# Convolution work kept out of the step that ends a run of the second matmul and the step behind it

## The chip, the cores and the metric

The kernel runs on one core of one Trainium2 chip. The metric is the device time of one execution in microseconds (us). Five engines work beside each other and meet through semaphores: TensorE (PE in the profile; PEld is its weight load), VectorE (DVE), ScalarE (ACT), GpSimd (POOL) and SyncE (SP, which issues the DMAs).

## What is computed

Two layers, each a gated long convolution (H3) and a squared-ReLU MLP, both behind a layernorm, on 2048 tokens of 1024 features, with 3584 hidden features, in float32:

```python
# x: [1, 2048, 1024]; layernorm over the features, no scale
def A(q, k, v, shift_k, ssm_k, ssm_D):
    kv = short_causal_conv(k, shift_k) * v          # 4 taps
    y = irfft(rfft(pad(kv)) * rfft(pad(ssm_k)))     # causal conv along the 2048 tokens, per feature
    return q * (y + kv * ssm_D)
def B(x, w1, b1, w2, b2):
    h = relu(x @ w1 + b1) ** 2
    return h @ w2 + b2
for _ in range(2):
    x = x + A(layernorm(x), k, v, shift_k, ssm_k, ssm_D)
    x = x + B(layernorm(x), w1, b1, w2, b2)
```

The convolution's result before the gate depends on k, v and the filter alone. It is the same for both layers, so it is computed once.

## The kernel before

**Matmuls.** The tokens are four blocks of 512. `ORDER` lists seven units of (layer, block): (0,0), (1,0), (0,1), (0,2), (1,1), (0,3), (1,2), the last of which takes blocks 2 and 3 of layer 1 together. A float32 product is three matmuls with a high and a low half of each operand (`mm3`, L355 to L358). The high half of a weight tile is a cast on ACT (L1112), the low half a subtraction on DVE or POOL (L1120), made some three steps ahead of its use; a hidden tile is treated the same way (L1599, L1602, L1604 on ACT, the low half at L1607 on DVE).

**Steps.** A unit is a list of steps. A step uses one weight tile: "m1" (first matmul) or "m2" (second). It has 12 matmuls of 512 columns, or of 256 columns where only half of the block's tokens are ready: the half steps at the turn from unit 0 to unit 1 are the last m2 steps of unit 0, from step 106, and the first m1 steps of unit 1, steps 134 to 157. Seven m2 steps make a run that sums in four PSUM banks. The last step of a run (`end`) is followed, one step later, by the eviction `evict` (L1727): four DVE additions into the sums in SBUF. At the turn, `add_b2` adds the second bias to the sums, four instructions on POOL (L1850).

**Convolution.** It is cut into blocks of 256 tokens and computed by a transform in short pieces. Its work is spread between the steps of units 0 to 4 in two ways:

- `fwd_tick` advances two generators. `fwd_x` makes one feature group's transform of the input: three shifted multiply-adds on DVE (L386), the product with v (L388), transposes on PE (L441) a fixed number of ticks later, then further matmuls and DVE combinations (L402, L423, L424, L428). `fwd_g` does the like for the filter (L485, L486, L489, L490, L504, L505).
- `prod_stream` (`pds`) makes the products of the transforms: a multiply on POOL (L546, by 3 to 8 blocks wide), a sum over it on DVE (L550), and for each group a fold (L696) and a butterfly (L700, L701) on POOL, then the inverse matmuls (L616) and a copy on ACT. Each call of `next(pds)` yields the work just issued in a unit of its own (0.384 for a product of 3 blocks, 0.512 for one of 4), or None where it waits for a forward transform or a buffer.

**Pacing.** In each step, `rate` is the work that should be issued (from `pace`), a tenth of it in half steps; `owed` sums it up. Products are issued until `todo`, at most 1.06 times the rate (`BURST`), is used up; one that is begun counts in full, so any `todo` above nothing issues one product. A None issues a forward tick instead. Beside that, `fowed` grows by `FWD_RATE` in each full step (1.4 in unit 0), and each whole one is a forward tick. No rule looks at whether a step ends a run. Every engine takes its instructions in the order in which the loop issues them.

Of the kernel before, what the change touches and what calls it, by code (L numbers as in the profile page):

```python
# [22 lines left out]
NT = T // P  # L23
# [24 lines left out]
W_AFTER = 4  # L48
AHEAD_0 = 4
BURST = 1.06  # L50
FIN = "GGG"
PACE_SLACK = {1: 74, 3: 10}
PACE_TO = {1: 2}
# [198 lines left out]
def tile_h3_mlp(ctx: ExitStack, tc: tile.TileContext, q, kT, vT, shk, ssmT, ssmD, w1, b1, w2, b2,  # L252
# [280 lines left out]
    def fwd_tick():  # L533
        for g in streams:
            next(g, None)
# [4 lines left out]
    def prod_stream():  # L540
# [11 lines left out]
        def fin(st, sm, sb, g, k):  # L552
            s = sm.rearrange("p k j c -> p k (j c)")
            E = ENG[FIN[sb - 1]]
            if k == 0:
# [1593 lines left out]
    owed = town = 0.0  # L2149
    fowed = 0.0  # L2150
# [3 lines left out]
    top = 0  # L2154
    cur_u = -1
    ready = set(ALL)

    def close_conv(nb):
        while nb not in done:
            if next(pds) is None:  # L2160
                fwd_tick()

    for s, (k, u, c, a, i, tts, w) in enumerate(steps):
# [58 lines left out]
        elif k == "w2":  # L2222
# [10 lines left out]
            if i == done_at - 1:  # L2233
                end = c == len(WCH) - 1
# [8 lines left out]
        else:  # L2243
            turned = direct[u] and c == NCH - 1 and tts[0] > 0 and a == 1
            begin, end = (s in opens, s in closes) if turned else (i == 0, i == FC - 1)
# [60 lines left out]
        rate = pace.get(u, 100) * (PREP_PACE if busy else 1.0)  # L2306
        if len(tts) < NT:
            rate *= 0.1
        owed += rate
        todo = min(owed, BURST * rate)  # L2310
        while todo > 0:
            x = next(pds, 0)
            if x == 0:
                owed = todo = 0
            elif x is None:
                fwd_tick()
                todo = 0
# [1 line left out]
                todo -= x  # L2319
                owed -= x  # L2320
        fowed += FWD_RATE.get(u, 2) * (0.0 if busy or len(tts) < NT else 1.0)
        while fowed >= 1:
            fowed -= 1
            fwd_tick()
    lag.flush()


# [47 lines left out]
```

## Time and profile before

| | us |
|---|---|
| time, median of 3 runs | 2676.86 (2676.43 to 2679.94) |
| the profiled execution | 2678.26 |
| its span in the trace | 2676.5 |
| granted clock of PE, mean | 0.995 |

How to read the profile: a row of the timeline gives the start, the duration, the engine, the line of the kernel, the operation, output and inputs, and in brackets how long the engine stood idle before it and what it waited for. A row of the groups by shape gives the count, then the total busy time and the mean duration in ns, then the idle time before the instructions of the group. The list of waits gives total us, times and the longest. A row of the windows gives the stretch, its length, then the busy time of each engine with the number of instructions, the granted clock of PE, the DMA engines' share and GB/s.

### The profile page before, as it was taken

The page shows a single profiled execution, that of the slowest core. Times are in us where ns is not written, and L with a number is a line of the kernel's source. Part 1 is how long each engine was busy: PE and PEld are TensorE (multiplying, and loading weights), DVE is VectorE, ACT ScalarE, POOL GpSimd, SP SyncE. Part 2 cuts the span into 40 slices and gives each one's busy share as a digit, 9 for nine tenths or more (in the row PEclk, how much of TensorE's full clock was granted, in tenths as well). Part 3 has the DMA queues.
Part 4 walks back from the last instruction along what each step waited for, and adds up shares of the span by engine and source line. Part 5 has one row for each costly group of instructions (what it writes and reads, how often), then busy time and mean ns, then how long its engine had stood idle before and what let it go on. Part 6 is the DMA issues. An engine that isn't in the chain of part 4 may idle for free.

```text
span 2676.5 us, 36110 instructions
## 1 busy us (share of the span) xinstructions
PE 2623.3 (98%) x12388; PEld 2198.9 (82%) x12388; DVE 1980.9 (74%) x2848; ACT 1133.8 (42%) x1931; POOL 1034.8 (39%) x683
## 2 busy tenths in 40 slices
PE   8899999899999999999999999999999999999999
PEld 7888787788888888888888888888788778888887
DVE  7878888789987777779777775456778767777553
ACT  5454344444444333343333422345444585454442
POOL 2436665255542645427554175000100217536111
PEclk9999999999999999999999999999999999999999
DMA  8799898689989998788987888689889798878653
GB/s 255 250 316 310 295 302 282 234 290 369 353 296 312 317 333 298 276 299 305 339 303 253 300 295 305 207 264 315 300 295 307 264 338 254 264 252 312 231 195 121
DMA packets 380265, 763.16 MB, mean 285 GB/s; under 512 B 44064, under 2 KB 159408, under 8 KB 377008
## 3 DMA queue, kind: packets, MB, share of 16 engines
q1 hardware_dynamic: 380080, 760.85, 83.3%
q8 instruction: 98, 1.61, 0.2%
q14 instruction: 87, 0.71, 0.1%
HBM read 583.49 MB, written 177.21 MB: 284 GB/s over the span
## 4 chain that ended last, share of the span: by engine, by line
PE 80%; DMA 6%; DVE 4%; ACT 2%; issue 1%; POOL 1%; SPq 0%; DVEq 0%; POOLq 0%; ACTq 0%
PE p L356 24%; PE p L357 24%; PE p L358 24%; PE pt L358 2%; PE pt L356 2%; PE pt L357 2%; DMA whl<-wd_m 2%; DMA wr<-w 1%; DMA wd_m<-whl 1%; DVE whl L1120 1%; DMA yt<-yd 0%; PE pt L412 0%; PE pt L441 0%; DMA cx<-xd 0%; PE pt L616 0%
## 5 line engine op out<-in xcount | busy, mean ns | idle before, releaser
L546 POOL TENSOR_TENSOR cp<-cx,cg 128x384 f32<-128x384 f32 (+5 forms) x288 | 542.6, 1897 | 569.2 <-DVE sm L550 374.6
L356 PE MATMUL p<-xh,whl 128*128 128x512 f32 (+1 forms) x1504 | 577.0, 384 | 6.3 <-DMA whl<-wd_m 5.7
L358 PE MATMUL p<-xh,whl 128*128 128x512 f32 (+1 forms) x1504 | 572.9, 381 | 3.3 <-DVE whl L1120 2.8
L357 PE MATMUL p<-xl,whl 128*128 128x512 f32 (+1 forms) x1504 | 572.8, 381 | 0.4 <-DVE xl L1515 0.4
L1112 ACT CAST whl<-wr 128x512 fp32r<-128x512 f32 x546 | 332.4, 619 | 466.4 <-PE p L358 275.1
L1120 DVE TENSOR_TENSOR whl<-wr,whl 128x512 fp32r<-128x512 f32 x486 | 426.2, 888 | 131.0 <-ACT whl L1112 130.3
L356 PE MATMUL p<-whl,rh 128*128 128x512 f32 x1204 | 477.1, 396 | 4.9 <-DMA whl<-wd_m 4.3
L357 PE MATMUL p<-whl,rh 128*128 128x512 f32 x1204 | 472.1, 392 | 2.5 <-POOL whl L1120 1.4
L358 PE MATMUL p<-whl,rl 128*128 128x512 f32 x1204 | 471.5, 392 | 0.0
L356 PEld LDWEIGHTS p<-xh,whl 128*128 128x128 f32 x1504 | 283.4, 188 | 61.1 <-DMA whl<-wd_m 2.5
L358 PEld LDWEIGHTS p<-xh,whl 128*128 128x128 f32 x1504 | 283.3, 188 | 58.3 <-DVE whl L1120 3.0
L357 PEld LDWEIGHTS p<-xl,whl 128*128 128x128 f32 x1504 | 283.5, 188 | 52.7 <-DVE xl L1515 0.6
L1607 DVE TENSOR_TENSOR rl<-wr,rh 128x512 fp32r<-128x512 f32 x140 | 142.2, 1016 | 177.9 <-ACT rh L1604 177.7
L356 PEld LDWEIGHTS p<-whl,rh 128*128 128x128 f32 x1204 | 227.9, 189 | 53.4 <-DVE fg L1716 3.3
L1120 POOL TENSOR_TENSOR whl<-wr,whl 128x512 fp32r<-128x512 f32 x60 | 87.3, 1458 | 475.9 <-ACT whl L1112 447.7
L357 PEld LDWEIGHTS p<-whl,rh 128*128 128x128 f32 x1204 | 227.9, 189 | 50.2 <-DVE whl L1120 2.7
L358 PEld LDWEIGHTS p<-whl,rl 128*128 128x128 f32 x1204 | 227.6, 189 | 48.0
L550 DVE TENSOR_REDUCE sm<-cp 128x128 f32<-128x384 f32 (+5 forms) x288 | 249.4, 874 | 10.2 <-POOL cp L546 10.2
L1599 ACT ACTIVATE wr<-p,b1t 128x512 f32<-128x512 f32 x138 | 95.3, 690 | 367.2 <-PE p L358 366.2
L1727 DVE TENSOR_TENSOR acc<-p,acc 128x512 f32<-128x512 f32 x152 | 100.0, 686 | 81.0 <-PE p L358 80.9
L696 POOL TENSOR_TENSOR sm<-sm 128x512 f32<-128x512 f32 x48 | 68.7, 1431 | 134.0 <-DVE sm L550 128.5
L356 PE MATMUL p<-whl,tq 128*128 128x512 f32 x276 | 107.4, 389 | 0.0
(393 smaller groups left out, 4280.5 us busy)
## 6 DMA issues: line engine op xcount, KB each, us to landing
whl<-wd_m SPq DMA_DIRECT2D x318, 512.0 KB, 5.5
wr<-w SPq DMA_DIRECT2D x442, 256.0 KB, 5.7
wd_m<-whl SPq DMA_DIRECT2D x70, 512.0 KB, 6.0
wr<-td SPq DMA_DIRECT2D x112, 256.0 KB, 5.0
cx<-xd SPq DMA_DIRECT2D x48, 512.0 KB, 5.9
cg<-gd SPq DMA_DIRECT2D x48, 512.0 KB, 6.8
tq<-hd SPq DMA_DIRECT2D x24, 1024.0 KB, 7.3
gd<-fg SPq DMA_DIRECT2D x72, 256.0 KB, 5.9
```

The lines of the kernel that those rows point to most:

```text
L356: PE.matmul(o, lh, rh, start=start, stop=False)
L357: PE.matmul(o, lh, rl, start=False, stop=False)
L358: PE.matmul(o, ll, rh, start=False, stop=stop)
L546: G.tensor_mul(pr.rearrange("p c i -> p i c"), xt[:, 0:j + 1], gt[:, j::-1])
L550: V.tensor_reduce(sm[:, ty, jj], st["pr"], axis=AX.X, op=OP.add)
L696: E.tensor_add(s[:, 1:3], s[:, 1:3], s[:, 0:1].to_broadcast([P, 2, s.shape[2]]))
L1112: A.copy(t[:, 0], raws[n]["t"])
L1120: ENG[e[n % len(e)]].tensor_sub(t[:, 1], raws[n]["t"], t[:, 0].bitcast(F32))
L1599: A.activation(r, st["o"], AF.Relu, bias=b1t[:, st["f"]:st["f"] + 1])
L1607: V.tensor_sub(st["lo"], st["r"]["t"], st["hi"].bitcast(F32))
L1727: V.tensor_add(accs[tt][:, d], o, accs[tt][:, d])
```

## The change

A new set `rest` holds the steps that follow the end of an m2 run. In the step that ends a run, and in the step behind it, nothing is issued from `pds`, and no forward tick is made. In the other full steps the limit is 1.3 times the rate instead of 1.06 where work is owed, and at most three forward ticks are made from `fowed`. In half steps the limit stays at 1.06 times their rate.

```diff
+CATCH = 1.3
...
+    rest = set()
...
         owed += rate
-        todo = min(owed, BURST * rate)
+        still = k == "m2" and end or s in rest
+        if k == "m2" and end:
+            rest.add(s + 1)
+        todo = 0.0 if still else min(owed, (BURST if len(tts) < NT else CATCH) * rate)
         while todo > 0:
             x = next(pds, 0)
             if x == 0:
                 owed = todo = 0
             elif x is None:
                 fwd_tick()
                 todo = 0
             else:
                 todo -= x
                 owed -= x
         fowed += FWD_RATE.get(u, 2) * (0.0 if busy or len(tts) < NT else 1.0)
-        while fowed >= 1:
-            fowed -= 1
-            fwd_tick()
+        for _ in range(0 if still else 3):
+            if fowed >= 1:
+                fowed -= 1
+                fwd_tick()
```

Each engine issues the same work in total; the order changes up to step 546, in unit 4, and is the same from there. Line numbers of the changed kernel are one higher than those of the kernel before in the rows below.

The first place is DVE in unit 0, at the product L388 (L389 after the change) of the fifth feature group, in step 58 before and step 59 now. Before, from the last eviction row of the run that ended in step 56:

```order
L1727 TENSOR_TENSOR acc_1357<-p2_2558,acc_1357 128x512
L1120 TENSOR_TENSOR whl_2769<-wr_2703,whl_2769 128x512
L550 TENSOR_REDUCE sm_2719<-cp_2790 128x128
L504 TENSOR_TENSOR fg_2834<-pt_2687,fg_2803 128x2x2x64
L505 TENSOR_TENSOR fg_2834<-pt_2687,fg_2803 128x2x2x64
L386 SCALAR_TENSOR_TENSOR fx_2832<-fx_2729,shkt_125,fx_2832 128x512 x3
L504 TENSOR_TENSOR fg_2840<-fk_2625 128x2x2x64
L505 TENSOR_TENSOR fg_2840<-fk_2625 128x2x2x64
L1120 TENSOR_TENSOR whl_2814<-wr_2740,whl_2814 128x512
L388 TENSOR_TENSOR fx_2832<-fx_2832,fx_2731 128x512
```

And now; the eviction of the same run, two L1121 and one L551 stand just ahead of the first row:

```order
L487 SCALAR_TENSOR_TENSOR pt_2695<-fk_2588,sgn_127,pt_2695 128x512
L490 SCALAR_TENSOR_TENSOR pt_2694<-pt_2695,fk_2589 128x512
L491 TENSOR_TENSOR pt_2695<-pt_2695,fk_2589 128x512
L505 TENSOR_TENSOR fg_2804<-pt_2695,fg_2801 128x2x2x64
L506 TENSOR_TENSOR fg_2804<-pt_2695,fg_2801 128x2x2x64
L1121 TENSOR_TENSOR whl_2771<-wr_2728,whl_2771 128x512
L505 TENSOR_TENSOR fg_2834<-pt_2694,fg_2801 128x2x2x64
L506 TENSOR_TENSOR fg_2834<-pt_2694,fg_2801 128x2x2x64
L505 TENSOR_TENSOR fg_2839<-fk_2589 128x2x2x64
L506 TENSOR_TENSOR fg_2839<-fk_2589 128x2x2x64
L387 SCALAR_TENSOR_TENSOR fx_2837<-fx_2795,shkt_125,fx_2837 128x512 x3
L389 TENSOR_TENSOR fx_2837<-fx_2837,fx_2797 128x512
```

The conv work has moved from the step behind the eviction to the two after it, with all of the filter's combinations of that group between the eviction and L387. On PE, the transposes of this product stood at the end of step 59, one step behind it; now they stand at the end of step 61, two steps behind it.

The second place is POOL at the start of unit 1, from the last of the four bias adds L1850 (L1851), in step 149. Here `cp` is a conv product, `whl` the low half of a weight tile and `sm` the sums of a group. Before:

```order
L1850 TENSOR_TENSOR acc_1357<-acc_1357,px_5150 128x1024
L1120 TENSOR_TENSOR whl_5277<-wr_5102,whl_5277 128x512
L546 TENSOR_TENSOR cp_5351<-cx_4432,cg_4433 128x4x128
L1120 TENSOR_TENSOR whl_5361<-wr_5297,whl_5361 128x512
L546 TENSOR_TENSOR cp_5417<-cx_4432,cg_4433 128x3x128
L546 TENSOR_TENSOR cp_5458<-cx_4432,cg_4433 128x4x128
L696 TENSOR_TENSOR sm_4553<-sm_4553 128x512
L700 TENSOR_TENSOR sm_4553<-sm_4553 128x256
L701 TENSOR_TENSOR sm_4553<-sm_4553 128x4x64
```

And now:

```order
L1851 TENSOR_TENSOR acc_1357<-acc_1357,px_5051 128x1024
L547 TENSOR_TENSOR cp_5179<-cx_4161,cg_4162 128x3x128
L547 TENSOR_TENSOR cp_5205<-cx_4161,cg_4162 128x4x128
L1121 TENSOR_TENSOR whl_5185<-wr_5003,whl_5185 128x512
L547 TENSOR_TENSOR cp_5236<-cx_4223,cg_4224 128x3x128
L547 TENSOR_TENSOR cp_5263<-cx_4223,cg_4224 128x4x128
L547 TENSOR_TENSOR cp_5281<-cx_4223,cg_4224 128x3x128
L547 TENSOR_TENSOR cp_5305<-cx_4223,cg_4224 128x4x128
L1121 TENSOR_TENSOR whl_5286<-wr_5220,whl_5286 128x512
L547 TENSOR_TENSOR cp_5334<-cx_5209,cg_5210 128x3x128
L547 TENSOR_TENSOR cp_5357<-cx_5209,cg_5210 128x4x128
L697 TENSOR_TENSOR sm_5178<-sm_5178 128x512
```

Behind these come one more product and the butterfly L701, L702 of `sm_5178`, whose inverse matmuls PE issues at the end of step 159. Two products stand ahead of the first L1121, where none stood, and four ahead of the second, where one stood; the inverse matmuls nearest to this place on PE stood in step 155 before, on sums that were finished long ahead, and the next in step 165.

## The prediction

> **What bounds the kernel now.** I read the page first: its busy times and its chain of work that ended last.
>
> ```profile
> span 2676.5 us, 36110 instructions
> PE 2623.3 (98%) x12388; PEld 2198.9 (82%) x12388; DVE 1980.9 (74%) x2848; ACT 1133.8 (42%) x1931; POOL 1034.8 (39%) x683
> PE 80%; DMA 6%; DVE 4%; ACT 2%; issue 1%; POOL 1%; SPq 0%; DVEq 0%; POOLq 0%; ACTq 0%
> ```
>
> PE is busy for 98% of the span and carries 80% of the chain. No matmul goes away, so only PE's idle time, and what the clock loses behind it, can be won. The windows say where that is (busy time of each engine in five stretches, then the granted clock):
>
> ```profile
> core 0: us, PE busy (x) PEld busy (x) DVE busy (x) ACT busy (x) POOL busy (x), PEclk, DMA share, GB/s
> 0.00:150.00 150.00, 133.28 (x863) 123.40 (x864) 110.37 (x166) 70.81 (x124) 49.45 (x53) 0.99 0.80 266
> 150.00:450.00 300.00, 289.99 (x1328) 242.24 (x1327) 260.46 (x369) 130.56 (x237) 173.31 (x134) 0.98 0.90 296
> 450.00:560.00 110.00, 101.68 (x602) 88.60 (x601) 83.42 (x138) 54.06 (x90) 43.76 (x29) 0.98 0.72 242
> 560.00:1692.00 1132.00, 1129.64 (x5304) 946.04 (x5303) 876.50 (x1172) 410.67 (x729) 542.83 (x298) 1.00 0.88 307
> 1692.00:2676.00 984.00, 968.68 (x4299) 798.68 (x4297) 650.11 (x1006) 467.71 (x751) 225.43 (x170) 1.00 0.79 264
> ```
>
> Up to the first run of the second matmul that ends, which lies in the second row, both kernels issue the same, and in both all conv work is issued by step 546, in unit 4; so the change can't reach the idle time of the first row and of the last. Between lie 300 - 290.0 = 10.0 us of idle PE in unit 0, 110 - 101.7 = 8.3 us at the turn from unit 0 to unit 1, and 2.4 us in all of units 1 to 4: there PE runs back to back, with nothing to be won, and a change of conv pacing can only lose. The list of what PE waited for names the stalls (total, times, longest):
>
> ```profile
> PE pt L441 <- DVE fx L388: 7.8, 4, 5.0
> PE pt L616 <- ACT whl L1112: 2.2, 1, 2.2
> PE p L358 <- DVE whl L1120: 2.8, 1, 2.8
> PE p L357 <- DVE whl L1120: 1.0, 2, 0.8
> PE p L358 <- POOL whl L1120: 0.5, 1, 0.5
> ```
>
> **What the change takes away in unit 0.** The largest of these is the transposes L441, issued a fixed number of conv ticks after the product L388. The timelines of PE at 260 and 300 us and of DVE ahead of the second one:
>
> ```profile
> 260.35 0.71 PE L441 MATMUL pt<-ident,fx 128*128 128x128 f32 x4 [2.18 <-DVE fx L388]
> ...
> 300.20 1.10 PE L441 MATMUL pt<-ident,fx 128*128 128x128 f32 x4 [4.98 <-DVE fx L388]
> ...
> 301.52 0.63 PE L357 MATMUL p<-whl,rh 128*128 128x512 f32 x1
> 301.95 0.63 PE L358 MATMUL p<-whl,rl 128*128 128x512 f32 x1
> ...
> 305.36 0.58 PE L357 MATMUL p<-whl,rh 128*128 128x512 f32 x1
> ...
> 307.60 0.39 PE L356 MATMUL p<-whl,rh 128*128 128x512 f32 x1
> 307.83 0.39 PE L357 MATMUL p<-whl,rh 128*128 128x512 f32 x1
> ```
>
> ```profile
> 287.54 2.48 DVE L1727 TENSOR_TENSOR acc<-p,acc 128x512 f32<-128x512 f32 x4
> ...
> 291.79 3.70 DVE L386 SCALAR_TENSOR_TENSOR fx<-fx,shkt 128x512 f32<-128x512 f32 x3
> ...
> 299.37 0.68 DVE L388 TENSOR_TENSOR fx<-fx 128x512 f32<-128x512 f32 x1
> ```
>
> The change takes this place apart. The eviction L1727 of the run that ended in step 56 and a whole conv block stand in one step, and the transposes one step behind. The stall costs 4.98 us and a tail: from 301.52 to 305.36 nine matmul starts lie 0.427 us apart instead of 0.227 (3.84 us for 9, against 307.60 to 307.83), so 1.8 us more. The 2.18 us stall at 260 has such a tail too; I take 1.5 for it and for the one on L616. That one comes at 445 us, behind the conv block of step 100, which moves to step 104, so it goes as well. Taken away: 2.2 + 5.0 + 2.2 of stalls and 1.8 + 1.5 + 1.5 of tails = **14.2 us**. The Trainium skill, "TensorE: Matmul & The Clock Gate" (What's actually happening), says the array falls to half clock only after an idle window of about 3.4 us. The trace disagrees in size, since the 0.427 us spacing follows a 2.18 us stall also; by the page's rule the tails would be dropped everywhere, and the sum below would come out about 0.5 us from where it does.
>
> **What it puts in their place.** With the ticks moved, L388 and L441 stand in steps 39 and 40, 48 and 50, 59 and 61, 71 and 72, 81 and 83, 92 and 95 (before: 36/38, 47/49, 58/59, 68/71, 79/81, 90/91). The trace shows two steps apart costing 0 to 2.18 us, and one step apart 0 (90/91) to 4.98. The new pair 39/40 stands right behind an eviction and the catch-up of three ticks: 2 us, 1.4 more than the 0.6 that is left of the row's 7.8 us for the pair 36/38 and 79/81 together. The pair 59/61 has one step more of PE (12 x 0.227 = 2.72 us) than 58/59 for the same DVE work: 4.98 - 2.72 = 2.3. The pair 71/72 is one step apart, with products at 1.3 times the rate ahead of it: between 0 and 5, I take 2.3. With a 1 us tail on each of the latter two: 1.4 + 3.3 + 3.3 = **+8.0**.
>
> Then the half steps. The conv block of the timeline
>
> ```profile
> 439.11 3.60 DVE L386 SCALAR_TENSOR_TENSOR fx<-fx,shkt 128x512 f32<-128x512 f32 x3
> 442.74 1.10 DVE L388 TENSOR_TENSOR fx<-fx 128x512 f32<-128x512 f32 x1
> ```
>
> (4.7 us, and six short L504/L505) moves from step 100 to 104, two steps ahead of the half steps of 1.36 us, which begin at 106. DVE enters them some 5 us later than now, and the low halves L1120 are made three steps ahead, now worth 3 x 1.36 = 4.1 us. Where DVE is on time PE waits 1.0 us there (the row of L357). Bounds: 0, if the block is worked off in step 105, and 5, if all of it shows. I take **+3 us**, tail included. Unit 0: -14.2 + 8.0 + 3 = **-3** (from -12 to +5).
>
> **What it costs at the turn.** Products not issued in still steps, and held up behind the forward transforms, leave four to six units owed at the half steps (before: about none). The limit there is a tenth of the rate, but a product is issued whenever the limit is above nothing: one in every half step from 151 to 157, and two in steps 158 to 162. They land on POOL right behind the bias adds L1850. POOL's timeline, PE's where it waits, and PE at the start of step 160:
>
> ```profile
> 533.10 10.87 POOL L1850 TENSOR_TENSOR acc<-acc,px 128x1024 f32<-128x1024 f32 x4
> 543.92 1.74 POOL L1120 TENSOR_TENSOR whl<-wr,whl 128x512 fp32r<-128x512 f32 x1
> 545.61 1.76 POOL L546 TENSOR_TENSOR cp<-cx,cg 128x512 f32<-128x512 f32 x1
> 547.33 1.75 POOL L1120 TENSOR_TENSOR whl<-wr,whl 128x512 fp32r<-128x512 f32 x1
> ```
>
> ```profile
> 545.72 0.39 PE L358 MATMUL p<-xh,whl 128*128 128x256 f32 x1 [0.53 <-POOL whl L1120]
> ...
> 553.89 0.39 PE L356 MATMUL p<-whl,rh 128*128 128x512 f32 x1
> ```
>
> and the groups by shape:
>
> ```profile
> L1120 POOL TENSOR_TENSOR whl<-wr,whl 128x512 fp32r<-128x512 f32 x60 | 87.3, 1458 | 475.9 <-ACT whl L1112 447.7 <-DVE rt L747 24.3 <-DMA whl<-wd_m 2.6
> L546 POOL TENSOR_TENSOR cp<-cx,cg 128x512 f32<-128x512 f32 x48 | 72.4, 1509 | 16.2 <-DVE sm L550 16.2
> L696 POOL TENSOR_TENSOR sm<-sm 128x512 f32<-128x512 f32 x48 | 68.7, 1431 | 134.0 <-DVE sm L550 128.5 <-DMA fg<-ssmT 4.3 <-DMA cg<-gd 1.3
> L546 POOL TENSOR_TENSOR cp<-cx,cg 128x384 f32<-128x384 f32 x48 | 59.5, 1239 | 74.7 <-DMA cg<-gd 67.7 <-DVE sm L550 4.3 <-DVE fy L424 1.5
> L700 POOL TENSOR_TENSOR sm<-sm 128x256 f32<-128x256 f32 x49 | 46.8, 955 | 5.1 <-DVE sm L696 4.4
> L701 POOL TENSOR_TENSOR sm<-sm 128x256 f32<-128x256 f32 x49 | 42.4, 865 | 3.8
> ```
>
> Already now PE waits for the L1120 that stands behind the adds. Now two products go in ahead of it: 543.97 + 1.24 + 1.51 + 1.46 = 548.2, 2.5 us later than its end at 545.7, and PE's wait grows by that. Then come four products, the next L1120, two products, the fold L696, one product and the butterfly L700/L701: 548.2 + 5.50 + 1.46 + 2.75 + 1.43 + 1.24 + 1.82 = 562.4 us. The inverse matmuls L616 at the end of step 159 read that butterfly. PE, delayed 2.5 us, is there at about 557, so it waits again, and step 160 starts at 562.4 + 4 x 0.23 = 563.3 instead of 553.9: 9.4 late. Off this go 1.5 us of conv matmuls that are done earlier than now; 1.5 of tails is added: **+9** (from +5, with POOL partly early, to +13, with every POOL instruction as long as the 1.74 to 1.76 beside DVE above). POOL catches up by step 165; the next inverse is issued there, behind it.
>
> **Units 1 to 4:** the moved ticks and products lie under PE at 1129.6 of 1132.0 us, and DVE is busy for 876.5 of it: 0, with -1 to +3 for ends. DMAs: the loads of cx and cg move with their products by a few steps, and no row above has PE waiting on them.
>
> **Sum:** 2678.3 (the profiled execution: 2676.5 of span and 1.8 around it) - 3 + 9 + 0 = 2684. That execution lies 1.4 us over the median of the runs, 2676.9, so I put the median after at **2683 us**, +0.2%.
>
> **Rivals.** *Slower outright:* DVE joins POOL in the half steps. The row
>
> ```profile
> 535.99 2.90 DVE L1120 TENSOR_TENSOR whl<-wr,whl 128x512 fp32r<-128x512 f32 x1
> ```
>
> shows a DVE instruction of 0.68 us at best taking 2.90 beside L1850. With a product on POOL in every half step, each two-input DVE instruction there takes as long as the POOL one beside it, and the fold waits for late sums. Then the turn costs +13, the stalls of 40, 61 and 72 eat unit 0's gain (0 instead of -3): 2676.9 + 13 = 2690. It decides if the L616 of step 159 starts after 564. The Trainium skill, "SBUF — State Buffer" (SBUF: two separate sides), states it as an exclusive lock on the port pair of VectorE and GpSimd, held for a whole instruction; 2.90 beside adds of 10.87 / 4 = 2.72 us agrees. *Faster:* the pairs 61 and 72 cost nothing, so unit 0 gives -11, and the products at the turn start early enough that only 3 us shows: 2669. Against it: POOL's order is fixed, and L1850 ends when it does. *No effect:* the evictions were never late outside unit 0, gain and loss both under 2 us: 2677.
>
> **How the numbers follow.** Forecast (net 0 to +9) 0.45; slower outright 0.25; faster 0.17; no effect 0.13. About 0.2%, 5.4 us, is what a measurement of this kernel can tell from no change; the bound, 2682.2, lies inside the forecast's case, so I split it 0.25 same and 0.20 slower. Slower: 0.20 + 0.25 = 0.45. Faster: 0.15 of 0.17. Same: 0.40. Range 2669 to 2694, from the faster case to somewhat beyond the slower one; the forecast's own range is 2677 to 2686.
>
> **What would show it.** L441 no longer waits at 260 and 300 but near steps 40, 61 and 72, 7 us in all; PE waits for POOL's L1120 3 us at 548 and for L616 some 5 us ahead of step 160; windows beyond 600 us unchanged. It is wrong if POOL's products at the turn don't delay L616, or if the half steps at 457 us stall for over 5 us.

## The result, and the profile after

| | before | after |
|---|---|---|
| median of 4 runs beside each other, us | 2678.15 | 2699.10 |
| the profiled execution, us | 2678.26 | 2700.37 |
| its span, us | 2676.5 | 2698.6 |

The ratio of the times is 1.0081, with a 95% interval of 1.0069 to 1.0094: the changed kernel is slower, by 21 us where 6 were forecast. The time lies 5 us above the range. One execution of e11 below, at 3274 us with a granted clock of 0.75, is left out of all that follows; every other execution had a clock of 0.99 or more. The head of the page, and its chain of work that ended last:

```profile
span 2698.6 us, 36105 instructions
PE 2628.7 (97%) x12388; PEld 2199.8 (82%) x12388; DVE 1972.1 (73%) x2848; ACT 1134.4 (42%) x1931; POOL 1027.5 (38%) x683
PE 74%; DMA 10%; DVE 5%; POOL 2%; ACT 2%; issue 1%; SPq 1%; DVEq 0%; POOLq 0%; ACTq 0%
```

No engine has more to do. PE gives 6 points of the chain away, and four of them go to DMA, which the prediction had set at nothing. The windows, between the same times as before except for the edge at 1700 (step 160 starts at 564.3 here and at 553.9 before):

```profile
core 0: us, PE busy (x) PEld busy (x) DVE busy (x) ACT busy (x) POOL busy (x), PEclk, DMA share, GB/s
0.00:150.00 150.00, 131.74 (x854) 121.92 (x855) 109.37 (x165) 70.70 (x124) 49.42 (x53) 0.99 0.80 263
150.00:450.00 300.00, 291.77 (x1344) 243.87 (x1342) 238.90 (x353) 128.02 (x230) 154.28 (x122) 0.99 0.86 286
450.00:560.00 110.00, 90.66 (x516) 78.32 (x517) 76.28 (x136) 50.89 (x86) 35.56 (x24) 0.91 0.68 232
560.00:1700.00 1140.00, 1130.86 (x5318) 945.46 (x5317) 891.69 (x1180) 412.49 (x732) 560.23 (x315) 1.00 0.88 308
1700.00:2698.00 998.00, 983.67 (x4362) 810.25 (x4360) 655.91 (x1017) 472.27 (x759) 227.98 (x171) 1.00 0.78 262
```

PE's idle time is 8.2 us in the second row (10.0 before), 110 - 90.66 = 19.3 in the third, with the half steps and the turn (8.3 before, and the granted clock there is 0.91 where it was 0.98), and 9.1 in the fourth, units 1 to 4 (2.4 before). The first and the last row are within 1.6 us of before. How far behind the kernel before each step starts says the same in us (the step's first matmul in both traces, after minus before):

| step | 14 | 106 | 110 | 134 | 150 | 160 | 330 | 546 |
|---|---|---|---|---|---|---|---|---|
| before, at | 145.5 | 456.8 | 462.2 | 503.2 | 533.8 | 553.9 | 1064.4 | 1692.4 |
| after | +1.1 | -4.4 | +2.8 | +1.8 | +1.4 | +10.4 | +23.6 | +22.2 |

The first matmul of step 106, the first half step, waits 3.97 us (below); without that wait the step would start 8.4 us earlier than before. So unit 0 up to the half steps wins 1.1 + 8.4 = 9.5 us, the entry into them costs 8.4 + 2.8 = 11.2, the turn between steps 150 and 160 costs 9.0, and units 1 and 2 up to step 330 cost another 13.2. Behind that the two keep their distance, within 1.4 us.

A part of this is work that has moved, and no wait. Counted by step, PE's trace has 28 matmuls of the convolution fewer than before between steps 14 and 106, 8 more between 150 and 160, 32 more between 160 and 330, and 12 fewer from there to 546. They start 0.11 to 0.12 us apart, so by this count that is about -3.1, +0.7, +3.8 and -1.4 us. So about 6.4 of unit 0's 9.5 us come from stalls and their tails, and about 9.4 us are lost between steps 160 and 546 beyond the work that moved.

PE's timeline shows each place: the pair of steps 71 and 72, three stalls at the entry into the half steps, the two at the turn, and the start of step 160.

```profile
338.78 1.13 PE L442 MATMUL pt<-ident,fx 128*128 128x128 f32 x4 [4.92 <-DVE fx L389]
...
452.42 0.79 PE L357 MATMUL p<-whl,rh 128*128 128x512 f32 x1 [3.97 <-ACT whl L1113]
454.08 0.79 PE L358 MATMUL p<-whl,rh 128*128 128x512 f32 x1 [0.87 <-DVE whl L1121]
...
459.46 0.50 PE L358 MATMUL p<-whl,rh 128*128 128x512 f32 x1 [2.45 <-DVE whl L1121]
...
460.72 0.63 PE L357 MATMUL p<-whl,rh 128*128 128x512 f32 x1
...
464.13 0.39 PE L359 MATMUL p<-whl,rl 128*128 128x512 f32 x1
...
549.31 0.38 PE L359 MATMUL p<-xh,whl 128*128 128x256 f32 x1 [1.68 <-POOL whl L1121]
...
555.35 0.80 PE L357 MATMUL p<-xh,whl 128*128 128x512 f32 x1 [4.60 <-DMA whl<-wd_m]
555.95 0.63 PE L358 MATMUL p<-xl,whl 128*128 128x512 f32 x1
...
559.36 0.55 PE L357 MATMUL p<-xh,whl 128*128 128x512 f32 x1
...
563.46 1.05 PE L617 MATMUL pt<-sm,yh 128*128 128x128 f32 x8
564.26 0.48 PE L357 MATMUL p<-whl,rh 128*128 128x512 f32 x1
```

The longest wait at the turn is on a transfer, the low half `whl` of a weight tile that comes ready-made from memory. The timeline of SP, whose queue issues it, says why it is late:

```profile
540.03 0.44 SPq L647 DMA_DIRECT2D cg<-gd  x1
547.61 0.32 SPq L647 DMA_DIRECT2D cx<-xd  x1
547.98 0.43 SPq L647 DMA_DIRECT2D cg<-gd  x1
548.45 0.43 SPq L1103 DMA_DIRECT2D wr<-w  x1
548.98 0.38 SPq L1109 DMA_DIRECT2D whl<-wd_m  x1
```

And POOL's, at the same time:

```profile
534.52 10.83 POOL L1851 TENSOR_TENSOR acc<-acc,px 128x1024 f32<-128x1024 f32 x4
545.31 2.28 POOL L547 TENSOR_TENSOR cp<-cx,cg 128x384 f32<-128x384 f32 x2
547.54 1.72 POOL L1121 TENSOR_TENSOR whl<-wr,whl 128x512 fp32r<-128x512 f32 x1
549.22 5.34 POOL L547 TENSOR_TENSOR cp<-cx,cg 128x384 f32<-128x384 f32 x4
...
562.19 0.74 POOL L702 TENSOR_TENSOR sm<-sm 128x256 f32<-128x256 f32 x1
```

SP issues nothing from 540.5 to 547.6 us. The load of the next `cx` may not start until the two products that read the old one are done; these stand behind the bias adds and end at 547.59. Behind that load, in the same queue, wait two weight loads, and PE needs the second: it is issued at 548.98 and PE starts at 555.35. In SP's list of waits (total, times, longest) the same thing shows over the whole kernel, here after:

```profile
SPq L647 <- POOL cp L547: 111.4, 38, 11.3
```

and here before:

```profile
SPq L646 <- POOL cp L546: 63.0, 30, 5.8
```

### The profile page after: what moved, and what is told of

It is laid out like the page before. It is cut to its first block, busy times and chain, and to the rows that moved or that the text cites. A ratio compares the mean times of both kernels' runs of the same rounds, so it can differ in the third digit from the quotient of the medians.

```text
span 2698.6 us, 36105 instructions
## 1 busy us (share of the span) xinstructions
PE 2628.7 (97%) x12388; PEld 2199.8 (82%) x12388; DVE 1972.1 (73%) x2848; ACT 1134.4 (42%) x1931; POOL 1027.5 (38%) x683
## 3 DMA queue, kind: packets, MB, share of 16 engines
q8 instruction: 98, 1.61, 0.2%
## 4 chain that ended last, share of the span: by engine, by line
PE 74%; DMA 10%; DVE 5%; POOL 2%; ACT 2%; issue 1%; SPq 1%; DVEq 0%; POOLq 0%; ACTq 0%
PE p L357 22%; PE p L359 22%; PE p L358 22%; PE pt L359 2%; PE pt L358 2%; PE pt L357 2%; DMA whl<-wd_m 2%; DMA wr<-w 2%; DMA wd_m<-whl 1%; DMA cg<-gd 1%; POOL acc L1851 1%; DVE whl L1121 1%; POOL cp L547 1%; DMA yt<-yd 1%; ACT whl L1113 0%
## 5 line engine op out<-in xcount | busy, mean ns | idle before, releaser
L547 POOL TENSOR_TENSOR cp<-cx,cg 128x384 f32<-128x384 f32 (+5 forms) x288 | 536.9, 1880 | 550.8 <-DVE sm L551 362.9
L1121 DVE TENSOR_TENSOR whl<-wr,whl 128x512 fp32r<-128x512 f32 x486 | 423.7, 883 | 123.3 <-ACT whl L1113 122.6
L1121 POOL TENSOR_TENSOR whl<-wr,whl 128x512 fp32r<-128x512 f32 x60 | 87.3, 1458 | 493.3 <-ACT whl L1113 444.4
L551 DVE TENSOR_REDUCE sm<-cp 128x128 f32<-128x384 f32 (+5 forms) x288 | 249.1, 875 | 30.7 <-POOL cp L547 30.1
L1608 DVE TENSOR_TENSOR rl<-wr,rh 128x512 fp32r<-128x512 f32 x140 | 150.3, 1074 | 156.2 <-ACT rh L1605 156.0
```

The costliest lines, as they stand in the source:

```text
L547: G.tensor_mul(pr.rearrange("p c i -> p i c"), xt[:, 0:j + 1], gt[:, j::-1])
L551: V.tensor_reduce(sm[:, ty, jj], st["pr"], axis=AX.X, op=OP.add)
L1121: ENG[e[n % len(e)]].tensor_sub(t[:, 1], raws[n]["t"], t[:, 0].bitcast(F32))
L1608: V.tensor_sub(st["lo"], st["r"]["t"], st["hi"].bitcast(F32))
```

## The experiments

Three questions were open: what makes the turn late, what makes units 1 and 2 late, which the sum had put at 0, and which part of the change is behind each. All diffs are against the changed kernel, but for the last two, which are against the kernel before. The table has the step starts of each run less those of the kernel before, in us, from their traces (a wait of the first matmul of step 106 is counted in its column), and the ratio of the times with its 95% interval. A single trace scatters: e12 issues the same as the kernel before up to step 158, and its trace is 3.7 us ahead at step 150. Differences between two columns hold better: the changed kernel and e6, which issue the same up to beyond step 160, lose 11.2 and 11.4 us at the entry and 9.0 and 8.6 at the turn.

| | 106 | 110 | 150 | 160 | 330 | ratio |
|---|---|---|---|---|---|---|
| after | -4.4 | +2.8 | +1.4 | +10.4 | +23.6 | 1.0081 (1.0069, 1.0094) |
| e1: conv loads issued by POOL | -7.9 | -0.1 | -1.8 | +9.7 | +32.3 | 1.0139 (1.0122, 1.0155) |
| e4: no products in half steps | -6.1 | +2.1 | -2.0 | -1.3 | +24.0 | 1.0074 (1.0057, 1.0091) |
| e9: bias adds spread | -10.0 | -2.0 | -5.9 | +0.1 | +15.1 | 1.0077 (1.0060, 1.0094) |
| e5: still steps from unit 1 on | -1.1 | -1.1 | +0.7 | +0.7 | +3.1 | 1.0016 (1.0006, 1.0025) |
| e6: still steps in unit 0 alone | -9.2 | -1.1 | -5.2 | +3.4 | +17.5 | 1.0060 (1.0045, 1.0075) |
| e2: limit 1.06 | -8.5 | -0.1 | -2.0 | +6.3 | +23.2 | 1.0081 (1.0060, 1.0101) |
| e7: ticks in every step | +0.3 | +0.6 | +7.4 | +15.7 | +26.2 | 1.0094 (1.0077, 1.0111) |
| e8: products in every step | -8.1 | -8.1 | -5.3 | -4.4 | +7.4 | 1.0046 (1.0031, 1.0061) |
| e10: e8, ticks still in unit 0 alone | -3.3 | -3.3 | -0.2 | +0.7 | +9.7 | 1.0043 (1.0030, 1.0055) |
| e11: before, L441 later | -3.3 | -3.2 | +3.3 | +3.2 | +10.9 | 1.0054 (1.0041, 1.0067) |
| e12: before, conv late in steps 158 to 167 | -2.7 | -2.7 | -3.7 | -5.2 | +9.8 | 1.0037 (1.0023, 1.0051) |

Between steps 160 and 330, 3.8 us of the loss are conv matmuls moved there in e1, e6 and e9, as in the changed kernel; 4.6 in e2 and e4, 2.9 in e7, 1.4 in e11 and e12, and none in e5, e8 and e10. The losses named below contain them.

### The turn

**e1: the loads of `cx` and `cg` are issued on POOL's queue**, so SP's weight loads stand behind no product.

```diff
-                SY.dma_start(t, src[g, :, :nb])
+                G.dma_start(t, src[g, :, :nb])
```

> The changed kernel (2699 us) with the loads of cx and cg (the conv products' inputs) issued from POOL's queue and not from SP's; all else stays. Theory A, SP's queue: these loads wait on SP until POOL has read the buffer, and the weight loads stand behind them; then PE's wait of 4.60 us at step 158 (named DMA whl<-wd_m) and that of 3.97 us at step 106 (named ACT whl, which had waited 11.66 us for DMA wr<-w) go or fall under 2 us each, SP's waits on POOL cp (111 us) go, and the time is 2683 to 2691. Theory B, POOL and DVE are themselves late at these places (the prediction's reason): the waits stay, under other names, and the time is 2695 or more.

Median 2714.1 us. The wait of 4.60 us on the weight load is gone, and the turn is no shorter: 11.6 us from step 150 to 160 (9.0 in the changed kernel). PE's timeline of this run:

```profile
456.72 0.79 PE L358 MATMUL p<-whl,rh 128*128 128x512 f32 x1 [3.21 <-DVE whl L1121]
...
547.79 0.39 PE L359 MATMUL p<-xh,whl 128*128 128x256 f32 x1 [3.42 <-POOL whl L1121]
...
561.96 1.38 PE L617 MATMUL pt<-sm,yh 128*128 128x128 f32 x5 [5.18 <-POOL sm L701]
```

At the entry 0.49 us are left of the stall on ACT's high half, and it costs 7.9 - 0.1 = 7.8 us instead of 11.2.

The last two rows are the waits that the prediction named, on POOL's low half and on the butterfly. In the changed kernel they are shortened or hidden by the wait for the weight load, which is late because the same products are. The changed kernel's own rows say the same: the butterfly ends at 562.19 + 0.74 = 562.93 us and PE's L617 starts at 563.46, so without the wait of 4.60 us PE would still have had to wait there, and could have won 0.5 us at most. The SP queue is where PE's wait shows, and not what sets the end of the turn. The run e1 isn't clean, as issuing costs POOL time; by its groups by shape,

```profile
L647 POOL DMA_DIRECT2D cx<-xd x144 | 80.9, 562 | 50.0 <-POOL cp L547 25.2 <-DMA xd<-fx 24.7
L647 POOL DMA_DIRECT2D cg<-gd x144 | 79.0, 549 | 4.9 <-DVE whl L1121 2.4 <-issue 2.4
```

288 loads keep POOL busy for 80.9 + 79.0 = 159.9 us, which can add to its lateness at the turn and to the 22.6 us that are lost between steps 160 and 330.

**e4: no products in the half steps of unit 1.** What is owed is issued in the full steps behind them.

```diff
-        todo = 0.0 if still else min(owed, (BURST if len(tts) < NT else CATCH) * rate)
+        todo = 0.0 if still or u and len(tts) < NT else min(owed, (BURST if len(tts) < NT else CATCH) * rate)
```

> The changed kernel with no products in the half steps of unit 1; what is owed there is issued from step 159 on, two products a step. Both theories: the 4.60 us wait at step 158 and its slow matmuls go, 6 to 8 us, and step 158 starts within 1 us of 2.5 us behind the kernel before. Theory A expects a part of it back behind step 160, as the loads still wait on SP for products issued two a step: 2692 to 2697. Theory B expects nothing back, since POOL has time there: 2690 to 2692.

Median 2697.8 us. The turn costs 0.8 us instead of 9.0: the owed products in the half steps are what made it late. But steps 160 to 330 now lose 25.3 us instead of 13.2, and the total is the same. What the turn wins is lost again behind it.

**e9: the four bias adds of unit 1 are issued in steps 149, 153, 157 and 161** instead of all in 149.

```diff
-    def add_b2(st, accs):
-        for a in accs:
+    def add_b2(st, accs, spread=0):
+        for n, a in enumerate(accs):
+            if spread and n:
+                lag.at(spread * n, lambda x: G.tensor_add(x, x, st["t"]), a)
+                continue
...
-                lag.at(16, add_b2, bst, accs)
+                lag.at(16, add_b2, bst, accs, 4 * (u == 1))
```

> The changed kernel with the four bias adds of unit 1 on POOL (10.8 us in a row at the turn) issued one in every fourth step, 149, 153, 157 and 161. If POOL's queue behind the adds sets the turn: PE's waits at 549 (1.7 us) and 555 (4.6 us) fall to 2 us together, step 160 starts some 5 us earlier, and the time is 2691 to 2696. If weight loads on SP are late for another reason: the 4.6 us wait stays, 2698 to 2701.

Median 2696.1 us (2688.9 to 2699.1; the profiled execution is the fastest of the four, so its trace shows less of the loss than the ratio). The waits of 1.68 and 4.60 us are gone, and one is left at the turn, again on the butterfly, as PE's timeline has it:

```profile
552.31 2.08 PE L617 MATMUL pt<-sm,yh 128*128 128x128 f32 x8 [4.16 <-POOL sm L701]
```

The turn costs 6.0 us instead of 9.0. So the adds ahead of the products make up part of it; with e4, the rest falls to the products.

### Unit 0 against the later units

**e5 and e6: still steps from unit 1 on, and in unit 0 alone.**

```diff
-        still = k == "m2" and end or s in rest
+        still = u > 0 and (k == "m2" and end or s in rest)
```

```diff
-        still = k == "m2" and end or s in rest
+        still = u == 0 and (k == "m2" and end or s in rest)
```

> The still steps only from unit 1 on; unit 0 and the turn are issued as before the change, and no products are owed at step 160. The changed kernel loses some 12 us between step 160 and unit 4. If still steps cost that by themselves (products pushed together behind each run of m2, SP's queue behind them): 2686 to 2691. If it is inherited from the products owed at the turn: 2677 to 2680, as before.

> The still steps only in unit 0, the other half of e5. Stage 0 and the turn as in the changed kernel (10 us behind at step 160). If the loss in units 1 to 4 comes from their own still steps: 2686 to 2689. If it is inherited: 2694 to 2699.

Medians 2680.1 and 2693.0 us. Still steps in units 1 to 4 alone cost 0.16%; those in unit 0 alone cost 0.60%, and the two add up to nearly the 0.81% of the whole change. In e6 the loss in steps 160 to 330 is 14.1 us, although nothing is kept still there. So units 1 and 2 lose most of that time through the state in which unit 0 hands the conv work over, not through their own still steps.

### Products, ticks and the limit

**e2: the limit back at 1.06.** **e7: only products are kept out of still steps. e8: only ticks are. e10: as e8, and ticks only in unit 0.** Their edits, in that order:

```diff
-CATCH = 1.3
+CATCH = 1.06
```

```diff
-        for _ in range(0 if still else 3):
+        for _ in range(3):
```

```diff
-        todo = 0.0 if still else min(owed, (BURST if len(tts) < NT else CATCH) * rate)
+        todo = min(owed, (BURST if len(tts) < NT else CATCH) * rate)
```

```diff
-        todo = 0.0 if still else min(owed, (BURST if len(tts) < NT else CATCH) * rate)
+        todo = min(owed, (BURST if len(tts) < NT else CATCH) * rate)
...
-        for _ in range(0 if still else 3):
+        for _ in range(0 if still and u == 0 else 3):
```

> The changed kernel with the limit of the other full steps back at 1.06 times the rate; 29 steps from 158 to 196 differ in when products are issued. If the products owed are held up by forward transforms that come late, and the limit is not what binds, this runs as the changed kernel: 2696 to 2701. If the faster catching up (two products a step behind the turn) is what crowds POOL: 2690 or less.

> The changed kernel with still steps for the products alone; forward ticks are made in every step again. Debt theory: the loss grows with the products owed at the turn, 5.7 units in the changed kernel (22 us), 3.0 here: 2685 to 2692. Rival, the place of the conv blocks beside evictions is what costs: 2679 or less, since the blocks are nearly back where they were.

> The other half: still steps for the forward ticks alone; products are issued in every step. No products are owed at step 134. Debt theory: turn and units 1 to 4 as before the change, 2674 to 2681. Rival as in e7: 2685 or more.

> The changed kernel with still steps for the forward ticks alone and in unit 0 alone; products are issued in every step, no products are owed at step 134, and units 1 to 4 pace themselves as before the change. In the run with ticks still everywhere, PE was 12 us ahead of the kernel before at step 103, 4.4 us ahead at 160, and lost 12 us in units 1 and 2. If that loss came from still ticks in units 1 and 2, the gain stays: 2670 to 2675, faster than before. If it came with any shift of the conv blocks by a few steps: 2679 to 2686.

Medians 2695.5, 2700.4, 2686.7 and 2688.2 us. The limit of 1.3 does nothing that can be measured: e2 has the same ratio as the change. With products in every step (e8, e10) the turn costs 0.9 us; with only the products held (e7), 8.3 us. So the held products make the turn late. The entry needs both: steps 106 to 110 cost nothing more in e7, e8 and e10, and a part of it comes later there (2.8 to 6.8 us from step 110 to 150). Between steps 160 and 330, though, all of them lose: 16.9 (e2), 10.5 (e7), 11.8 (e8) and 9.0 us (e10). e8 and e10 owe next to nothing at the end of unit 0. The idea that the loss there grows with what is owed falls with them. More than half of the loss is one wait, with slow starts behind it, in e10; in PE's timeline it is

```profile
695.15 0.58 PE L357 MATMUL pt<-fg,fh 128*128 128x256 f32 x1 [4.71 <-DVE fy L425]
```

and DVE's timeline shows what stands ahead of that L425, the high and low parts of an inverse transform (L583):

```profile
690.70 3.20 DVE L583 TENSOR_TENSOR yl<-sm,yh 128x256 fp32r<-128x256 f32 x2
693.82 0.68 DVE L424 TENSOR_TENSOR fy<-pt,fx 128x512 f32<-128x512 f32 x1
694.42 0.68 DVE L425 TENSOR_TENSOR fy<-pt,fx 128x512 f32<-128x512 f32 x1
```

Between L425's end, at 695.10, and PE's start nothing else lies: DVE's own queue is what PE waits for here. The same wait of PE on L425 stands in e8, 4.79 us at 696.76, and in e6, 5.14 us at 762.08; there too L583 is ahead of it on DVE. Why the shifted ticks bring the two together is not shown.

### From the kernel before

**e11: the transposes L441 of the kernel before come one tick later** for the token block `sb == 1`, five ticks behind the product instead of four, without still steps.

```diff
-        for _ in range(4 if sb == 1 else 7):
+        for _ in range(5 if sb == 1 else 7):
```

> The kernel before with the transposes of the first forward blocks five ticks behind the product L388 in place of four, and nothing of the change. The pair that cost 4.98 us stands three steps apart and not one, the pair 47/49 becomes 48/50; no products are owed at step 134. If those stalls can be had without moving work into the turn: 2668 to 2674. If DVE's lateness shows elsewhere in unit 0 or the shifted blocks cost in unit 1: 2676 or more.

Median 2691.3 us, of four executions. It wins 3.5 us from step 14 to 110, gives 6.5 back by step 150, and loses 7.7 more between steps 160 and 330.

**e12: in the kernel before, no conv work is issued in steps 158 to 167, and what it owes is made up later** at the old limit of 1.06.

```diff
-        todo = min(owed, BURST * rate)
+        held_back = 158 <= s < 168
+        todo = 0.0 if held_back else min(owed, BURST * rate)
...
-        fowed += FWD_RATE.get(u, 2) * (0.0 if busy or len(tts) < NT else 1.0)
+        fowed += FWD_RATE.get(u, 2) * (0.0 if busy or held_back or len(tts) < NT else 1.0)
```

> The kernel before with no products and no forward ticks in steps 158 to 167, and nothing of the change; 6.4 units are owed at step 180 (7.0 in the changed kernel), and the products L388 stand at 173, 187, 203, 217 and 235, within two steps of the changed kernel's. Unit 0 and the turn are as before. If late conv work by itself costs the 9 us that the changed kernel loses in units 1 and 2: 2683 to 2688. If that loss needs the still steps or the turn: 2675 to 2679.

Median 2689.0 us, 1.0037 times the kernel before. Up to step 158 it issues what the kernel before does, and steps 160 to 330 lose 15.0 us in the trace. The stretch from step 160 to 330 in the windows of the kernel before,

```profile
552.00:1066.00 514.00, 513.38 (x2445) 431.42 (x2444) 425.81 (x592) 200.65 (x361) 248.12 (x151) 1.00 0.94 326
```

of the changed kernel,

```profile
562.00:1090.00 528.00, 520.60 (x2485) 435.75 (x2484) 435.99 (x606) 203.17 (x366) 268.05 (x166) 1.00 0.92 321
```

and of e12:

```profile
548.00:1076.00 528.00, 519.45 (x2452) 435.26 (x2452) 409.82 (x588) 200.47 (x361) 243.71 (x153) 0.99 0.91 316
```

PE is idle for 0.6, 7.4 and 8.6 us. The rest of the loss in the changed kernel is mostly the 32 conv matmuls moved there, 3.8 us; only one matmul there starts 0.4 us or more ahead of the next without a wait between. In e12 fifteen do, 3.1 us, and 1.4 us are moved conv matmuls. The stalls are not the same ones. In the changed kernel they are ten of at most 1.3 us, the largest at 618.64 on DVE's L1121 and at 718.61 on DVE's L403. In e12 two make up most of it:

```profile
653.53 0.76 PE L356 MATMUL p<-whl,rh 128*128 128x512 f32 x1 [3.80 <-DMA whl<-wd_m]
...
906.61 0.58 PE L356 MATMUL pt<-fx,fh 128*128 128x256 f32 x1 [3.29 <-ACT fx L400]
```

Late conv work alone is enough to lose 10 us by the ratio, with no still steps at all.

## Why the prediction was wrong

The sign of the forecast time was right, and the size was off by 16 us: 2699.1 against 2683.

**What the change takes away in unit 0: right.** The stalls at 260, 300 and 445 us are gone. Up to the entry unit 0 wins 9.5 us, where 14.2 - 8.0 = 6.2 were forecast; about 3.1 of it are conv matmuls that PE does later, which the sum left out, and about 6.4 are what was forecast.

**The pairs put in their place: right in sum, wrong in parts.** Steps 39/40 cost 0.46 us (forecast 1.4), 59/61 next to nothing (3.3), and 71/72 a stall of 4.92 us with its tail where 3.3 were put. PE's list of waits has them in one row:

```profile
PE pt L442 <- DVE fx L389: 5.6, 3, 4.9
```

**The entry into the half steps: mis-sized, and half of it not seen.** It was put at +3 us with a bound of 5, and a stall of over 5 was named as a sign of being wrong. It cost 11.2 in four half steps (of six matmuls of 512 columns each, not twelve): three waits of 3.97 + 0.87 + 2.45 = 7.3 us, and half speed behind them. The two on DVE's L1121, 3.3 us, are the term that was put there. The first and longest, on ACT's high half, stood in no term. ACT's timeline shows that ACT had itself waited for the weight tile:

```profile
451.75 0.62 ACT L1113 CAST whl<-wr 128x512 fp32r<-128x512 f32 x1 [11.66 <-DMA wr<-w]
```

and SP's why its load was late:

```profile
430.55 0.43 SPq L647 DMA_DIRECT2D cg<-gd  x1
442.08 0.32 SPq L647 DMA_DIRECT2D cx<-xd  x1
...
446.56 0.42 SPq L1103 DMA_DIRECT2D wr<-w  x1
```

From 431.0 to 442.1 us SP waits for a product on POOL, and the weights `wr` come behind. Here the step on the DMAs failed: "no row above has PE waiting on them" was true of the trace before, whose longest such wait of SP was 5.8 us, and said nothing of products that are held back while a load waits for their buffer. With e1, where SP waits for no product, all but 0.49 us of the stall on ACT's tile are gone and the entry costs 3.4 us less. Of the 7.8 that are left, 1.61 + 3.21 = 4.8 are waits on DVE's L1121, and the whole is still more than the 5 of the bound.

**The turn: right in size, and only partly in mechanism.** Forecast +9, measured 9.0. The butterfly was put at 562.4 and ends at 562.19 + 0.74 = 562.9; step 160 was put at 563.3 and starts at 564.26. L1121 was put 2.5 us later, and PE waits 1.68 for it. So POOL's queue sets the end of the turn, as forecast. But PE does not wait at L617: a weight load behind `cx` on SP's queue holds it for 4.60 us first. By e1 that wait can go and the named ones come out, 3.42 and 5.18 us; by e4 and e8 the products in the half steps are the cause of both. The rival "slower outright", with DVE joining POOL, is not what happened: no wait for DVE stands between steps 150 and 160, and L617 starts at 563.46, not after 564. The 1.5 us of conv matmuls that the sum took off are not there either; the trace has 0.7 us more of them.

**Units 1 to 4: the step that failed.** "The moved ticks and products lie under PE at 1129.6 of 1132.0 us, and DVE is busy for 876.5 of it: 0, with -1 to +3 for ends." Between steps 160 and 546 they cost 11.8 us, of which 11.8 - 3.8 + 1.4 = 9.4 are no moved work. Without these 9.4 the time would be 2690 us, inside the range. The reason given for the 0 was two averages, and they hide the tight places. DVE's 876.5 of 1132 us are 77%, but a window on the kernel before shows

```profile
614.00:660.00 46.00, 45.38 (x216) 37.79 (x215) 45.76 (x58) 19.38 (x34) 27.05 (x16) 1.00 1.04 377
```

45.76 us of DVE in 46. e12 shows that conv work a few steps late loses as much with no other edit, e6 that most of the loss comes from how unit 0 ends and not from the still steps in units 1 to 4, e11 that a move of one tick in unit 0 is enough for 7.7 us. So the step that put moved work under PE at no cost is what failed. That a full DVE hands the delay on is a guess. For it speak the rows of e10, e8 and e6. Against it speaks that the changed kernel has a stretch as full as that one, and PE is not idle in it at all:

```profile
628.00:674.00 46.00, 46.00 (x216) 38.51 (x215) 45.86 (x52) 20.18 (x36) 34.42 (x20) 1.00 1.03 381
```

e12 also has DVE less busy between steps 160 and 330 (409.8 us), and its stalls are on a transfer and on ACT. What they have in common stays open.

None of the versions beats the kernel before; the nearest is e5, at 1.0016.

## What to carry to other kernels

A busy share over a long stage doesn't show that work moved into it is free. Here the stage had 77% of DVE and no idle PE, which leaves nothing to win and everything to lose, and every version that shifted conv work in unit 0 lost 8 to 25 us between steps 160 and 330, at most 4.6 of them in conv matmuls moved there. Put such a term at a range that can only cost, not at 0. Before a gain is put down to a stall that went away, count what the limiting engine still has to do in that stretch: 3.1 of unit 0's 9.5 us were only work done later. For every transfer behind a moved instruction, ask what stands behind it in the queue that issues it, since a load that waits for its buffer holds all later loads of that queue. When the one wait that the trace names is taken away, expect another that was as late: in e1 the wait of 4.60 us went and the turn got no shorter.

## What the hardware showed

- A load issued from POOL's queue kept POOL busy for 0.55 to 0.56 us each (the rows of e1), 160 us for 288 of them.
- Matmuls run 0.427 us apart instead of 0.227 not only behind the stall of 4.60 us (555.95 to 559.36 in the timeline, eight starts) but also behind the one of 2.45 us at the entry, where eight starts lie so up to 464.13. The slow starts there begin at 460.72, 1.3 us after the stall's end. The Trainium skill, "TensorE: Matmul & The Clock Gate" (What's actually happening), has an idle window of about 3.4 us for it; these rows, like the 2.18 us of the kernel before, put it lower, or several stalls count together. The length of the stall alone doesn't decide it: in e10 eight such starts follow a stall of 1.90 us at 226.05, with no other stall in the 8 us ahead of it, and in e11 none follow one of 2.90 us at 450.28. What does is open.
